# Two more one-class gemm1 blocks in the fill list, a later start for the last output projection, and a guard on pulling class-0 tiles

## The chip, the cores and the metric

The kernel runs on one core of a Trainium2 chip. The metric is device time in microseconds (us) of one execution. Five engines work side by side, each through its own queue in order: TensorE (PE, with its weight loads as PEld), VectorE (DVE), ScalarE (ACT), GpSimd (POOL) and SyncE (SP, which here only issues DMAs). A tile framework inserts the semaphores; it also lists the instructions of each engine, by the order in which the program emits them where they are ready in its own reckoning.

## The reference

Two kinds of layer alternate, twice each, on x of 2048 positions by D = 1024 (bf16):

```python
x = x + A(layernorm(x), wqkv, wo)        # attention, 32 heads of 32
x = x + B(layernorm(x), w1, b1, w2, b2)  # MLP across positions, F = 3584
...
# A: each position attends to W = 8 positions, a distance dil = 2 apart:
idx = pos[:, None] - dil * arange(8)[None, :]
logits = einsum("bhsd,bhswd->bhsw", q, k[idx]) * scale    # masked where idx < 0
o = einsum("bhsw,bhswd->bhsd", softmax(logits), v[idx])   # then o @ wo
# B: normalises x again, then mixes the positions of each channel:
u = gelu(einsum("bsd,sf->bdf", layernorm(x), w1) + b1)
y = einsum("bdf,fs->bds", u, w2) + b2                     # then transposed back
```

## The kernel before, in words

Because the window has a step of 2, the even positions ("class 0") and the odd ones ("class 1") never meet in attention. Each class has 1024 rows, that is 8 tiles of 128. One pass of the loop over `li` ("layer 0", "layer 1" below) does an attention layer and the MLP that follows.

**Attention.** TensorE projects q, k and v (`project`, L410) and ScalarE copies them out of PSUM (L414, L417). For each chunk n of four 128-row groups (chunks 0 and 1 are class 0, chunks 2 and 3 class 1) VectorE multiplies q by shifted k into a tile T (`qk`, L442), TensorE sums over the head with 8 narrow matmuls ("sc", L447), `softmax_front` and `softmax_back` follow, a DMA spreads the probabilities into `pb`, and VectorE forms the weighted sum of v in `pv` (L503 to L509), whose result is oT. T tiles share 2 buffers, so a third T waits for the sc matmuls of the first.

**Output projection.** `out_proj` multiplies oT by wo for 8 tiles, each in two PSUM banks (n = 0, 1) of 8 matmuls (kt = 0 to 7; L629); VectorE adds the residual and so frees the bank (L650 or L653), POOL writes the row tile to `xa`, and the tile is normalised into h2. wo comes in four DMAs of 512 KB (L619). For class 1 the first three tiles are begun early: kt 0 to 5 of all three, which fills the 6 banks of the pool `psp`, then kt 6 and 7 tile by tile.

**gemm1.** The 3584 columns of w1 are 14 blocks (`fb`) of 256, each in 4 units (2 column tiles by 2 halves of D). A unit over one class is 8 matmuls (L680), over both 16. Blocks 0 to NPART-1 = 9 are done class by class: the class-0 partial sum is copied to g by ScalarE (L686), and later VectorE adds the class-1 sum to it (L691) before the gelu (L692). Blocks 10 to 13 take both classes at once (gelu straight from PSUM, L688). The g of blocks 6 to 13 lie in the memory of v of class 1 (`v_g`). A class of a block needs its own w1 tile (L667, 512 KB). w1, w2, wo and some wqkv tiles share the five buffers of `wbp`. `gemm2_tile` (L704, L709) does the second MLP product.

**Order around the change.** `weave` writes the order. The `lead` is the attention stream and then `out_proj` of class 1. The `fills` are class-0 `out_proj` ("out0"), the class-0 partials of gemm1 blocks 0 to 5 ("partials") and of blocks 6 to NPART-1 ("late"), besides `second` and `v_ahead`. `weave` keeps two planned clocks, `pe` and `dve`; each unit says its cost. Before a lead unit that needs TensorE at time t, `reach(t)` pulls fill units until pe is within SLACK = 0.5 of t or none is open. A DVE unit of the lead also pulls one out0 tile (3.5 of pe) whenever another OUT0_GAP = 7.0 of DVE cost has gone by. What is left of the fills is pulled after the lead. Early class-1 accumulation waits, by the entry `("less", "oT", -6.0)`, until pe is at the planned end of the last `pv` plus 6.

Of the kernel before, what the change touches and what calls it, by code (L numbers as in the profile page):

```python
# [13 lines left out]
BF16 = mybir.dt.bfloat16  # L14

P = 128
# [3 lines left out]
DIL = 2  # L20
# [6 lines left out]
def kernel(  # L27
# [13 lines left out]
    nc = tc.nc  # L41
# [3 lines left out]
    F = B_w1.shape[1]  # L45
    KD = D // P
    FT = F // P
    SC = S // DIL
    NT = SC // P
    HT = SC // 2  # L50
    NDC = D // 512
# [8 lines left out]
    FB = 256  # L60
    NFB = F // FB
    GF = FB // P
    NPART = 10
    NW2 = 4
    HF = FT // NW2
    SLACK = 0.5
    PB_LAG = 12.0
    PDW = 4 * SB * W * TB + 512
    OUT0_GAP = 7.0
    assert D == H * DH and W == 8 and SC == 1024 and HD * KD == H and SB * CH == 32  # L70
    scale = float(DH) ** -0.5

    def pool(name, bufs, **kw):
        return ctx.enter_context(tc.tile_pool(name=name, bufs=bufs, **kw))
# [8 lines left out]
    tpl = pool("tpl", 2)  # L83
    pbp = pool("pbp", 2)
    otp = pool("otp", KD)
    dram = pool("dram", 1, space=bass.MemoryType.DRAM)
# [19 lines left out]
    def bank(name="ps"):  # L106
        return psp.tile([P, 512], FP32, name=name, tag="ps")
# [4 lines left out]
    def hx(name, shape):  # L112
        return hxp.tile(shape, BF16, name=name, tag="hx")

    def wb(name, shape):
        return wbp.tile(shape, BF16, name=name, tag="wb")
# [53 lines left out]

    xa = [[dram.tile([SC, D], BF16, name=f"xa{li}{c}") for c in range(DIL)] for li in range(2)]
    xb = [dram.tile([SC, D], BF16, name=f"xb{c}") for c in range(DIL)]
    pd = [dram.tile([CH, PDW], BF16, name=f"pd{n}") for n in range(2 * DIL * NCQ)]

    xin_v = x_in.rearrange("(i m c) d -> c i m d", m=P, c=DIL)
# [6 lines left out]
    def rows(t):  # L182
        return t.rearrange("(i m) d -> i m d", m=P)
# [425 lines left out]
    def out_proj(at_, c, res, dst, h2, on_act):  # L609

        early = 0 if on_act else 3
        if early:
            yield "pe", 1.28 * early * NDC, [("oT", 0), ("less", "oT", -6.0)], [], 0.0
        dst_v = rows(dst)
        wo_t = [[None, None] for _ in range(NDC)]
        for n in range(NDC):
            for hf in range(2):
                wt = wb("wo", [P, KD // 2, 512])
                nc.sync.dma_start(out=wt[:], in_=wo_v[hf, :, :, n * 512:(n + 1) * 512])  # L619
                wo_t[n][hf] = wt  # L620
        for hf in range(2):
            h2[c][hf] = hx(f"h2{c}{hf}", [P, NT // 2, D])
        banks = {}

        def multiply(i, n, kts):
            if (i, n) not in banks:
                banks[(i, n)] = bank()
            for kt in kts:
                nc.tensor.matmul(banks[(i, n)][:], lhsT=at_.oT[c][kt][:, i * P:(i + 1) * P],  # L629
                                 rhs=wo_t[n][kt // 4][:, kt % 4, :], start=(kt == 0), stop=(kt == KD - 1))  # L630

        def kts(i):
            return range(KD - 2 if i < early else 0, KD)

        for i in range(early):
            for n in range(NDC):
                multiply(i, n, range(KD - 2))
        xrs = Rows([res[i] for i in range(NT)], 2)
        for i in range(NT):
            if early:  # L640
                yield "pe", 0.43 * len(kts(i)), ["oT"], [], 3.6
                on_act = i % 2 == 0
            xn = xrs.take()
            s1 = st("s1", [P, NDC]) if on_act else None
            for n in range(NDC):
                cols = slice(n * 512, (n + 1) * 512)
                multiply(i, n, kts(i))
                ps = banks.pop((i, n))
                if on_act:
                    nc.vector.scalar_tensor_tensor(out=xn[:, cols], in0=ps[:], scalar=1.0, in1=xn[:, cols], op0=ALU.mult,  # L650
                                                   op1=ALU.add, accum_out=s1[:, n:n + 1])
                else:
                    nc.vector.tensor_tensor(out=xn[:, cols], in0=ps[:], in1=xn[:, cols], op=ALU.add)  # L653
            nc.gpsimd.dma_start(out=dst_v[i], in_=xn[:])
            h = h2[c][i // 4][:, i % 4, :]
            if on_act:
                nm, rs = stats_act(xn[:], 1.0 + EPS, eps2, h, s1)
                norm_act(h, xn[:], nm, rs)
            else:
                mean, rs = stats_dve(xn[:], 1.0 + EPS, eps2)  # L660
                norm_dve(h, xn[:], mean, rs)
            if not early:
                yield 3.5, 0.0
# [31 lines left out]
    def gemm2_tile(c, i, w2t, xs, dst, hT, on_act=False, end=False):  # L695
        xo = xs.take()
        halves = [slice(n * 512, (n + 1) * 512) for n in range(NDC)]
        groups = [halves[:1], [slice(512, 768)], [slice(768, 1024)]] if end else [halves]
        for cols in groups:
            acc = [bank() for _ in cols]  # L700
            for n in range(NW2):
                for ft in range(n * HF, (n + 1) * HF):
                    for ps, xc in zip(acc, cols):
                        nc.tensor.matmul(ps[:, 0:xc.stop - xc.start], lhsT=w2t[n][:, ft % HF, c::DIL],  # L704
                                         rhs=g[ft // GF][:, ft % GF, xc], start=(ft == 0), stop=(ft == FT - 1))
                if n < NW2 - 1:
                    yield 1.5 * len(cols), 0.0
            for ps, xc in zip(acc, cols):
                nc.vector.scalar_tensor_tensor(out=xo[:, xc], in0=ps[:, 0:xc.stop - xc.start], scalar=b2_sb[:, i, c:c + 1],  # L709
                                               in1=xo[:, xc], op0=ALU.add, op1=ALU.add)  # L710
            yield 1.5 * len(cols), 0.75 * len(cols)
            if end:
                nc.sync.dma_start(out=dst[:, cols[0]], in_=xo[:, cols[0]])
        if not end:
            nc.gpsimd.dma_start(out=dst, in_=xo[:])
        if hT is None:
            return
        hb = x2("hb")
        if on_act:
            nm, rs = stats_act(xo[:], 1.0, eps1, hb[:])  # L720
            norm_act(hb[:], xo[:], nm, rs)
        else:
            mean, rs = stats_dve(xo[:], 1.0, eps1)
            norm_dve(hb[:], xo[:], mean, rs)
        to_hT(hb[:], hT, c, i)
        yield 0.0, 0.0 if on_act else 2.0

    def w2_tiles(i):
        tiles = []
        for n in range(NW2):  # L730
            t = wb("w2", [P, HF, FB])
            nc.sync.dma_start(out=t[:], in_=w2_v[:, n * HF:(n + 1) * HF, i * FB:(i + 1) * FB])
            tiles.append(t)
        return tiles

    def run(*its):
        for _ in chain(*its):
# [2 lines left out]
    def weave(lead, fills, lags):  # L740


        pe = dve = due = 0.0
# [32 lines left out]
        for kind, *unit in lead:  # L776
            if kind == "open":
                after = {"out0": "oT", "partials": "out0", "late": "out0", "v_ahead": "second"}.get(unit[0])
                opened[unit[0]] = when.get(after, float("inf")) if after else pe
            elif kind == "drain":  # L780
                while unit[0] in opened:
                    pull(True)
            elif kind == "at":
                pe, dve = unit
            elif kind == "pe":
                cost, waits, sets, then = unit
                reach(ready(pe, waits))
                pe += cost
                when.update((x, pe + 2.0) for x in sets)
                if then:  # L790
                    dve = max(dve, pe) + then
            else:
                cost, waits, sets, lag, then = unit
                dve = ready(dve, waits) + cost
                if then:
                    reach(dve)
                    pe += then
                when.update((x, dve + lag) for x in sets)
                if list(opened)[:1] == ["out0"] and opened["out0"] < pe:
                    due += cost  # L800
                    if due > OUT0_GAP:
                        due -= OUT0_GAP
                        pull()
        while pull(True):
# [4 lines left out]
    for li in range(2):  # L809
# [39 lines left out]
        def partials(lo, hi):  # L849
            for fb in range(lo, hi):  # L850
# [4 lines left out]
                     "out0": out_proj(at_, 0, res[0], xa[li][0], h2, on_act=True),  # L855
                     "partials": partials(0, NFB - KD), "late": partials(NFB - KD, NPART)},
              {"second": 25.0} if first else {})
        for fb in range(NPART, NFB):
            run(gemm1(h2, fb, (0, 1), True, True))
        for fb in range(NPART):  # L860
            run(gemm1(h2, fb, (1,), False, True))
# [8 lines left out]
        else:  # L870
            xs = Rows([rows(xa[1][c])[i] for i in range(NT) for c in range(DIL)], 1)
            for i in range(NT):
                w2t = w2_tiles(i)
# [32 lines left out]
```

## Time and profile before

| | |
|---|---|
| median of 3 runs | 1305.59 us (1304.1 to 1305.82) |
| profiled execution, its own time | 1303.7 us |
| its span, first to last instruction | 1301.9 us |
| PE busy | 1274.3 us (98%), 6284 matmuls |
| DVE busy | 669.5 us (51%) |
| ACT busy | 463.9 us (36%) |
| mean granted TensorE clock | 0.997 |
| DMA | 173.00 MB, mean 133 GB/s |

The span has a part for layer 0 up to about 575 us and one for layer 1 after it. In the timeline each row gives start, duration, engine, line, operation, output<-input and the number of instructions merged; a bracket says how long the engine was idle before it and what released it. In a table of windows each engine has its busy time in the stretch and, in brackets, its number of instructions; PEclk is the granted share of TensorE's full clock.

### The profile page before, as it was taken

The page shows a single profiled execution, that of the slowest core. Times are in us where ns is not written, and L with a number is a line of the kernel's source. Part 1 is how long each engine was busy: PE and PEld are TensorE (multiplying, and loading weights), DVE is VectorE, ACT ScalarE, POOL GpSimd, SP SyncE. Part 2 cuts the span into 40 slices and gives each one's busy share as a digit, 9 for nine tenths or more (in the row PEclk, how much of TensorE's full clock was granted, in tenths as well). Part 3 has the DMA queues.
Part 4 walks back from the last instruction along what each step waited for, and adds up shares of the span by engine and source line. Part 5 has one row for each costly group of instructions (what it writes and reads, how often), then busy time and mean ns, then how long its engine had stood idle before and what let it go on. Part 6 is the DMA issues. An engine that isn't in the chain of part 4 may idle for free. (4 is left out here: it accounts for less than half of the span.)

```text
span 1301.9 us, 15529 instructions
## 1 busy us (share of the span) xinstructions
PE 1274.3 (98%) x6284; PEld 575.2 (44%) x6284; DVE 669.5 (51%) x845; ACT 463.9 (36%) x788; POOL 60.8 (5%) x166
## 2 busy tenths in 40 slices
PE   8999999998999999999999999999999999999999
PEld 4344444443444444444444444444444444444444
DVE  6879899988003423335896734879920044011011
ACT  6845447634313410024414535475352244000000
POOL 3000001001000000000000000010000000000000
PEclk9999999998999999999999999999999999999999
DMA  9843436653422268753659772338252321434331
GB/s 257 181 121 97 106 105 170 172 136 107 135 66 81 75 156 225 213 144 109 165 160 239 188 203 65 90 122 226 81 172 62 92 81 57 135 112 131 113 112 53
DMA packets 243544, 173.00 MB, mean 133 GB/s; under 512 B 32208, under 2 KB 227152, under 8 KB 241424
## 3 DMA queue, kind: packets, MB, share of 16 engines
q1 hardware_dynamic: 233648, 133.45, 38.1%
q0 software_dynamic: 9248, 37.51, 10.2%
q8 instruction: 49, 0.80, 0.3%
q10 hardware_dynamic: 576, 1.05, 0.2%
q14 instruction: 23, 0.19, 0.0%
HBM read 146.81 MB, written 18.87 MB: 127 GB/s over the span
## 5 line engine op out<-in xcount | busy, mean ns | idle before, releaser
L704 PE MATMUL ps<-g,w 128*128 128x512 bf16 (+1 forms) x1820 | 390.7, 376 | 3.4 <-ACT v L417 2.2
L680 PE MATMUL ps<-h,w 128*128 128x512 bf16 x1792 | 388.9, 379 | 4.3 <-ACT h L231 3.0
L704 PEld LDWEIGHTS <-w 128*128 128x128 bf16 x1820 | 177.4, 98 | 215.0 <-issue 6.9
L680 PEld LDWEIGHTS <-w 128*128 128x128 bf16 x1792 | 175.0, 98 | 217.4 <-issue 6.0
L410 PE MATMUL ps<-hT,wq 128*128 128x512 bf16 (+1 forms) x1112 | 243.4, 375 | 3.5 <-DVE xr L709 2.2
L691 DVE TENSOR_TENSOR tmp<-ps,g 128x512 f32<-128x512 f32 x80 | 55.4, 692 | 232.8 <-PE ps L680 232.8
L709 DVE SCALAR_TENSOR_TENSOR xr<-ps,b_sb,xr 128x512 bf16<-128x512 f32 (+1 forms) x65 | 45.6, 737 | 251.7 <-PE ps L704 211.8
L442 DVE TENSOR_TENSOR T<-q,k 128x4096 bf16<-128x4096 bf16 x60 | 135.5, 2285 | 63.5 <-ACT q L414 52.9
L410 PEld LDWEIGHTS <-wq 128*128 128x128 bf16 x1112 | 108.4, 100 | 133.1 <-issue 15.0
L507 DVE TENSOR_TENSOR pr<-pr 128x2048 bf16<-128x2048 bf16 (+1 forms) x128 | 119.1, 945 | 0.2
L410 PE MATMUL ps<-hT,wv 128*128 128x512 bf16 x448 | 101.8, 380 | 0.0
L629 PE MATMUL ps<-wo,oT 128*128 128x512 bf16 x384 | 90.5, 382 | 1.6 <-DMA wo<-in_A_wo_dram 1.6
L417 ACT CAST k<-ps 128x1024 bf16<-128x1024 f32 x60 | 60.8, 1015 | 76.6 <-PE ps L410 74.6
L503 DVE TENSOR_TENSOR pr<-pb,v 128x2048 bf16<-128x2048 bf16 x64 | 76.0, 1215 | 23.2 <-DMA pb<-pd 13.5
L692 ACT ACTIVATE g<-tmp,b_sb 128x512 bf16<-128x512 f32 x80 | 57.7, 722 | 82.1 <-DVE tmp L691 82.1
L503 DVE TENSOR_TENSOR pr<-pb,g 128x2048 bf16<-128x2048 bf16 x64 | 76.2, 1212 | 9.0 <-DMA pb<-pd 9.0
L686 ACT CAST g<-ps 128x512 bf16<-128x512 f32 x80 | 45.8, 591 | 73.3 <-PE ps L680 73.3
L410 PEld LDWEIGHTS <-wv 128*128 128x128 bf16 x448 | 48.6, 112 | 50.5 <-issue 7.2
L629 PEld LDWEIGHTS <-oT 128*128 128x128 bf16 x384 | 37.4, 98 | 48.7 <-issue 5.1
L688 ACT ACTIVATE g<-ps,b_sb 128x512 bf16<-128x512 f32 x32 | 22.0, 687 | 83.2 <-PE ps L680 83.2
L414 ACT CAST q<-ps 128x512 bf16<-128x512 f32 x60 | 34.8, 584 | 46.7 <-PE ps L410 46.7
L417 ACT CAST g<-ps 128x1024 bf16<-128x1024 f32 x36 | 36.6, 1017 | 40.6 <-PE ps L410 40.6
(90 smaller groups left out, 597.6 us busy)
## 6 DMA issues: line engine op xcount, KB each, us to landing
w<-in_B_w_dram SPq DMA_DIRECT2D x96, 448.0 KB, 3.7
w<-in_B_w_dram SPq DMA_DIRECT2D x56, 512.0 KB, 4.5
wq<-in_A_wqkv_dram SPq DMA_DIRECT2D x38, 512.0 KB, 4.2
pb<-pd POOLq DMA_DIRECT2D x16, 1024.0 KB, 10.1
wo<-in_A_wo_dram SPq DMA_DIRECT2D x16, 512.0 KB, 5.1
xa<-xr POOLq DMA_DIRECT2D x32, 256.0 KB, 3.3
xr<-xa SPq DMA_DIRECT2D x32, 256.0 KB, 3.6
wv<-in_A_wqkv_dram SPq DMA_DIRECT2D x14, 512.0 KB, 6.9
```

The source lines that it names most:

```text
L410: nc.tensor.matmul(ps[:, lo:hi], lhsT=cols, rhs=self.hT[c][hf][:, kt, lo:hi], start=(kt == 0), stop=(kt == KD - 1))
L417: nc.scalar.copy(out=window(buf, 0, PADK + hf * HT, [(KW + 1, 2), (1, HT)]), in_=ps[:].unsqueeze(1).to_broadcast([P, 2, HT]))
L442: nc.vector.tensor_tensor(out=T[:], in0=q.unsqueeze(1).to_broadcast([P, 4, SC]), in1=window(k, par, 2, [(2, 4), (1, SC)]), op=ALU.mult)
L503: nc.vector.tensor_tensor(out=pr[:, :, u, :], in0=pb[:, :, u, :], in1=window(self.v_of(c, dt), par, 2 + hf * HT, [(TB, 4), (2, 4), (1, TB) ...
L507: nc.vector.tensor_tensor(out=pr[:, :, 0:wd, :], in0=pr[:, :, 0:wd, :], in1=pr[:, :, wd:2 * wd, :], op=ALU.add)
L629: nc.tensor.matmul(banks[(i, n)][:], lhsT=at_.oT[c][kt][:, i * P:(i + 1) * P], rhs=wo_t[n][kt // 4][:, kt % 4, :], start=(kt == 0), stop=( ...
L680: nc.tensor.matmul(ps[:], lhsT=wt[c][:, i, fl * P:(fl + 1) * P], rhs=h2[c][i // 4][:, i % 4, dc * 512:(dc + 1) * 512], start=(k == 0), sto ...
L686: nc.scalar.copy(out=gs, in_=ps[:])
L691: nc.vector.tensor_tensor(out=tmp[:], in0=ps[:], in1=gs, op=ALU.add)
L692: nc.scalar.activation(out=gs, in_=tmp[:], func=ACT.Gelu_apprx_tanh, bias=b1_sb[:, ft:ft + 1])
L704: nc.tensor.matmul(ps[:, 0:xc.stop - xc.start], lhsT=w2t[n][:, ft % HF, c::DIL], rhs=g[ft // GF][:, ft % GF, xc], start=(ft == 0), stop=(f ...
L709: nc.vector.scalar_tensor_tensor(out=xo[:, xc], in0=ps[:, 0:xc.stop - xc.start], scalar=b2_sb[:, i, c:c + 1], in1=xo[:, xc], op0=ALU.add, ...
```

## The change

Three things act. NPART becomes 12, so blocks 10 and 11 of gemm1 are done class by class as well, in both layers, and their class-0 partials join the "late" fills; only blocks 12 and 13 take both classes at once. The wait of the early class-1 accumulation is for the planned end of the last `pv` plus 12, no longer plus 6. And a class-0 output tile that is due in a DVE unit of the lead is not pulled while pe is AHEAD = 10 or more ahead of dve; it stays due, and the next DVE unit asks again.

The rest doesn't act: gemm2 takes its w2 slice through a function that gives the same slice as before, and `keep`, `w2_kept` and the DRAM tiles `w2_odd` are defined but no caller uses them (the calls of `w2_tiles(i)` in L840, L869 and L873 are as they were).

```diff
-    NPART = 10
+    NPART = 12
...
     OUT0_GAP = 7.0
+    AHEAD = 10.0
...
+    w2_odd = [dram.tile([P, F], BF16, name=f"w2o{i}") for i in range(NT)]
...
         if early:
-            yield "pe", 1.28 * early * NDC, [("oT", 0), ("less", "oT", -6.0)], [], 0.0
+            yield "pe", 1.28 * early * NDC, [("oT", 0), ("less", "oT", -12.0)], [], 0.0
...
-                        nc.tensor.matmul(ps[:, 0:xc.stop - xc.start], lhsT=w2t[n][:, ft % HF, c::DIL],
+                        nc.tensor.matmul(ps[:, 0:xc.stop - xc.start], lhsT=w2t(ft, c),
...
-    def w2_tiles(i):
+    def w2_tiles(i, keep=False):
         tiles = []
+        odd = tpl.tile([P, NW2, HF, P], BF16, name="odd", tag="T") if keep else None
         for n in range(NW2):
             t = wb("w2", [P, HF, FB])
             nc.sync.dma_start(out=t[:], in_=w2_v[:, n * HF:(n + 1) * HF, i * FB:(i + 1) * FB])
+            if keep:
+                nc.scalar.copy(out=odd[:, n], in_=t[:, :, 1::DIL])
             tiles.append(t)
-        return tiles
...
+        return lambda ft, c: tiles[ft // HF][:, ft % HF, c::DIL]
+
+    def w2_kept(i):
...
                 if list(opened)[:1] == ["out0"] and opened["out0"] < pe:
                     due += cost
-                    if due > OUT0_GAP:
+                    if due > OUT0_GAP and pe < dve + AHEAD:
                         due -= OUT0_GAP
                         pull()
```

More of the change, by code (lines that the diff above doesn't have):

```diff
@@ L732, in w2_tiles @@
             nc.sync.dma_start(out=t[:], in_=w2_v[:, n * HF:(n + 1) * HF, i * FB:(i + 1) * FB])
+            if keep:
+                nc.scalar.copy(out=odd[:, n], in_=t[:, :, 1::DIL])
             tiles.append(t)
-        return tiles
+        if keep:
+            nc.scalar.dma_start(out=w2_odd[i].rearrange("p (f m) -> p f m", m=P), in_=odd[:].rearrange("p n f m -> p (n f) m"))
+        return lambda ft, c: tiles[ft // HF][:, ft % HF, c::DIL]
+    def w2_kept(i):
+        tiles = []
+        for n in range(2):
+            t = wb("w2", [P, FT // 2, P])
+            nc.sync.dma_start(out=t[:].rearrange("p f m -> p (f m)"), in_=w2_odd[i][:, n * F // 2:(n + 1) * F // 2])
+            tiles.append(t)
+        return lambda ft, c: tiles[ft // (FT // 2)][:, ft % (FT // 2), :]
     def run(*its):
```

## The prediction

> **What bounds the kernel now.** I read the page first: PE is busy 98% of the span. The rest, 1301.9 - 1274.3 = 27.6 us, and time lost to a lower clock is all that an edit which adds and removes no matmul can win. This one has 6284 before and after: a gemm1 block has 4 x 16 matmuls whether it takes the classes together or apart. So I looked for where PE stands, in a table of windows:
>
> ```profile
> 290.00:300.00 10.00, 9.36 (x44) 4.13 (x43) 10.00 (x12) 0.00 (x0) 0.00 (x0) 1.00 0.00 0
> 300.00:310.00 10.00, 5.97 (x18) 2.31 (x18) 9.49 (x22) 5.15 (x13) 1.67 (x3) 0.66 0.20 59
> ...
> 880.00:890.00 10.00, 9.19 (x43) 4.00 (x41) 10.00 (x17) 5.21 (x12) 1.74 (x3) 1.00 0.99 270
> 890.00:900.00 10.00, 8.24 (x40) 3.63 (x38) 7.38 (x9) 7.26 (x15) 1.05 (x2) 1.00 0.80 210
> ```
>
> (Busy us and count of PE, PEld, DVE, ACT, POOL; then PEclk, DMA share, GB/s.) Two places lie in what `weave` orders. At 300 us, in layer 0, PE is idle and then has a clock of 0.66. At 880 to 893, in layer 1, it has small gaps. The others (the opening, q/k/v of layer 0, 675 to 775) lie ahead of anything that changes in their layer.
>
> PE's timeline at the first, with DVE's:
>
> ```profile
> 296.17 3.19 PE L629 MATMUL ps<-wo,oT 128*128 128x512 bf16 x14
> 304.03 1.87 PE L629 MATMUL ps<-wo,v 128*128 128x512 bf16 x4 [4.67 <-DVE xr L650]
> 305.69 1.91 PE L629 MATMUL ps<-wo,oT 128*128 128x512 bf16 x4
> 307.39 1.59 PE L629 MATMUL ps<-wo,v 128*128 128x512 bf16 x4
> 308.82 1.03 PE L629 MATMUL ps<-wo,oT 128*128 128x512 bf16 x4
> ...
> 326.35 18.95 PE L680 MATMUL ps<-h,w 128*128 128x512 bf16 x87 [0.96 <-DMA w<-in_B_w_dram]
> ```
> ```profile
> 302.94 0.42 DVE L509 TENSOR_TENSOR oT<-pr 128x512 bf16<-128x512 bf16 x1
> 303.28 0.69 DVE L650 SCALAR_TENSOR_TENSOR xr<-ps,xr 128x512 bf16<-128x512 f32 x1
> ```
>
> The three early class-1 tiles fill all 6 PSUM banks. They are done by 299.4, but the evictions that free the banks stand in DVE's queue behind the last `pv`, which ends at 303.3. Tile 3 waits 4.67 us for a bank. Only work put ahead of the early tiles fills that time: a unit of gemm1 needs a bank too.
>
> At the second place (PE, DVE, ACT):
>
> ```profile
> 885.05 2.75 PE L680 MATMUL ps<-h,w 128*128 128x512 bf16 x12 [0.47 <-ACT h L231]
> 888.14 3.18 PE L680 MATMUL ps<-h,w 128*128 128x512 bf16 x14 [0.34 <-DVE xr L650]
> 893.08 32.54 PE L680 MATMUL ps<-h,w 128*128 128x512 bf16 x150 [1.76 <-ACT h L231]
> ```
> ```profile
> 864.86 0.69 DVE L650 SCALAR_TENSOR_TENSOR xr<-ps,xr 128x512 bf16<-128x512 f32 x1 [1.03 <-PE ps L629]
> ...
> 865.49 4.49 DVE L442 TENSOR_TENSOR T<-q,k 128x4096 bf16<-128x4096 bf16 x2
> ```
>
> PE has begun gemm1 in all its banks and waits for h2 of the last class-0 tile, written on ACT at 893.0. The chain of waits leads back from there through ACT and a DVE without a gap to the T at 867.7. Ahead of that, at 852 to 865, DVE waited 9.3 us for PE in 8 pieces: four class-0 output tiles stood in PE's queue ahead of the sc matmuls that free T's buffers.
>
> **The later start (+12 for +6), with NPART.** `weave` pulls units of 8 x 0.216 = 1.728 of pe until pe is within 0.5 of the target. In layer 0 its clocks stand at pe 245.0 and dve 292.2 after the last `pv`: (292.2 + 6 - 0.5 - 245.0) / 1.728 = 30.5, so 31 units. The trace has 248 L680 matmuls ahead of the early tiles, which is 31 x 8, so this arithmetic can be trusted for order. With 12: 33.97, so 34 units. In layer 1 (pe 326.4, dve 359.7; one unit is drained earlier) 24 become 27, three of them block 6 from "late"; 192 matmuls in the trace confirm the 24. So 3 more units, 3 x 8 x 0.216 = 5.18 us of PE work, go ahead of the early tiles in each layer.
>
> Layer 0: the early tiles begin at 288.83 + 5.18 = 294.0 and PE asks for tile 3's bank at 299.36 + 5.18 = 304.54. DVE frees it at 303.97 as before. The stall of 4.67 us goes, with 0.5 us to spare. After it 12 matmuls took 304.03 to 308.82, 4.79 us, where 12 x 0.216 = 2.59 was due: 2.20 us more. [...] By the row the place is worth 4.67 + 2.20 = 6.87 us[...]. I take the row, since my sum is against this execution[...]. Next late is DVE, 6 evictions behind, but a tile takes DVE some 2.5 us (2 x 0.69, and 2.1 more for every other tile) against 3.46 on PE. Tile 4's residual comes at about 308.6 + 3.2 = 311.8, and the bank that waits for it isn't asked for before 318. PE stays fed.
>
> Weight DMAs. The fourth wo tile takes the buffer of a w1 tile that ends 2 units, 3.46 us, before the early start (before: 3 units; its DMA at 283.8 landed in 3.7). It is used 10 matmuls, 2.2 us, into the early tiles: 5.6 us of time against 3.7. I take 0. With the slowest landing of the four, 11.2, it is 5.6, a bound I think far: that one met `pb` traffic, this one runs alone. After class 1's last tile PE waited 0.96 us for w1, since one unit was left of the block at hand. Now two are left, 1.73 us more: -0.96. In layer 1 the roles change: 27 units leave just one, where 24 ended a block whose successor's w1 had long been loaded. I take the same 0.96 there, as +0.96 (0 to 2). In layer 1 nothing else waited but some 0.15 us at 935.98 for a bank, which goes: -0.15.
>
> **NPART's other half.** Per layer 8 units more go through ACT's copy (8 x 0.59 = 4.7 us) and DVE's add (8 x 0.69 = 5.5 us), with the w1 loads the same in number. They lie in stretches in which PE has 1.73 us per unit against 0.69 of DVE and 0.72 + 0.59 of ACT, and PE shows no gap from 345 to 550. Taken at 0; without that cover 8 x 1.3 = 10 us per layer. Blocks 10 and 11 overwrite v that the last `pv` has read long before.
>
> **AHEAD.** By the planner's clocks a gate needs pe 10 ahead of dve at a pull. Layer 0's widest is 219.1 against 210.1, 9.0: nothing changes. Layer 1 has 291.7 against 277.6 and, later, 299.3 against 289.2: two pulls are put off by one DVE unit each, and tile 3 falls behind the first sc group of chunk 3's second half. On PE that group moves up by one tile, 16 x 0.216 = 3.46 us, from 864.8 to about 861.3; its T has been ready since 848. The next T begins at about 862 in place of 865.5; the one after is held by tile 3 and the second sc group until about 865.8, where it stood at 867.7. So DVE's tight run begins 1.8 us earlier, less up to 1 us if it then stands for tile 4's second bank at 870.0. I take 1.2, and as that run sets h2, PE's gaps fall from 2.57 to 1.4. Both sides: -2.57 (gaps gone) to +2 (the framework lists DVE's work otherwise and h2 comes later). The moved tiles' xr loads on SP and xa writes on POOL go with them and stand ahead of the pb writes as before.
>
> **Sum.** Layer 0: -6.87 - 0.96 = -7.83. Layer 1: -1.2 - 0.15 + 0.96 = -0.4. Together -8.2. The profiled execution, 1303.7 (span 1301.9 and 1.8 around it), becomes 1295.5. It was 1.9 below the median of the runs; on the median I predict 1305.6 - 8.2 = 1297.4.
>
> **Rivals.** About 0.2%, 2.6 us, is what a measurement of this kernel can tell from none.
> 1. [...]4.67 + 0.96 + 0.4 = 6.0 to 7, so 1299.
> 2. The place at 300 takes a new wait. For: a wo tile's landing reached 11.2; then 5.6 of 6.87 comes back, and 1303.0 to 1304 remains. Against: 3.7 on the quiet queue.
> 3. Layer 1 wins all its gaps and w1 comes in time: another 1.4 + 0.96, so 1295.
> 4. Slower: the gate postpones DVE's evictions. If both postponed tiles push the last class-0 eviction behind one more `pv` unit each (2 x 4.4 us, by the row spacing of `pv` at 904 to 935), h2 comes 8.8 us later, and PE, with its banks all begun, stands over 11 us and loses 2.2 to the clock: -8.2 + 1.2 + 8.8 + 2.2 = +4, 1309.6. It decides where h2 is over 7.4 us late. Against: the late pulls catch up by the second T, ahead of DVE's tight run.
> 5. The units don't go ahead since the framework lists them elsewhere: 1305. Against: 31 and 24 hold.
>
> **How the numbers follow.** Forecast (with 1) 0.68, rival 3 0.10, rival 2 and 5 together 0.13, rival 4 0.09. Faster 0.78, within 0.2% 0.13, slower 0.09. The range runs from rival 3, with 1 us of spread, to the faster edge of rival 2: 1294 to 1303.
>
> **What would show it.** Right: 272 and 216 L680 matmuls ahead of the early tiles, no wait on L650 over 1 us and a clock of 1.00 near 305, the T run of layer 1 beginning near 862, a w1 wait of about 1 us after layer 1's projection and none in layer 0. Wrong: a wait on wo near 296, h2 of layer 1 later than 893, or a PE gap in gemm1's class-1 pass.

## The result, and the profile after

The changed kernel takes 1296.56 us in the median (1295.91 to 1298.79, 4 runs) against 1304.96 for the kernel before (1304.1 to 1305.82, 4 runs). The ratio is 0.9939, 95% interval 0.9921 to 0.9956: faster by 8 us. The forecast was 8.2. A second group of runs, beside other kernels, gave 0.9941 (0.9928 to 0.9953).

The same windows of the profile after, with the columns as in the prediction. The lines of the code have moved by 2, so L629 is now L631, L650 is L652 and L680 is L682:

```profile
290.00:300.00 10.00, 9.95 (x47) 4.53 (x47) 10.00 (x12) 2.34 (x4) 0.00 (x0) 1.00 0.18 52
300.00:310.00 10.00, 9.95 (x48) 4.51 (x47) 9.96 (x21) 3.59 (x8) 1.13 (x2) 1.00 0.14 52
870.00:880.00 10.00, 8.96 (x42) 3.99 (x41) 9.91 (x17) 7.42 (x15) 0.88 (x2) 1.00 0.91 261
880.00:890.00 10.00, 9.59 (x45) 4.29 (x45) 9.28 (x13) 7.37 (x16) 1.92 (x4) 1.00 0.79 222
```

At 300 us PE is full and its clock is 1.00. Windows that read 9.95 are full as well: this trace lacks some matmul records (6163 of 6284), so counts are taken from PEld. A table for the gemm1 line alone (PE, PEld, then clock, DMA share, GB/s), up to the early class-1 tiles of each layer, shows how many matmuls now lie ahead of them:

```profile
220.00:295.30 75.30, 59.23 (x266) 26.34 (x272) 1.00 0.56 150
845.00:922.50 77.50, 46.70 (x212) 21.13 (x216) 1.00 0.59 164
```

There are 272 and 216 weight loads, that is 34 and 27 units, as forecast. PE's timeline at the place where it stood idle, and at its end:

```profile
302.65 3.19 PE L631 MATMUL ps<-wo,oT 128*128 128x512 bf16 x14
305.68 1.03 PE L631 MATMUL ps<-wo,v 128*128 128x512 bf16 x3
306.54 1.03 PE L631 MATMUL ps<-wo,oT 128*128 128x512 bf16 x4
...
322.94 22.39 PE L682 MATMUL ps<-h,w 128*128 128x512 bf16 x101
```

Tile 3 follows the early tiles without a bracket, and gemm1 follows the last tile without one. In layer 1:

```profile
877.77 6.85 PE L682 MATMUL ps<-h,w 128*128 128x512 bf16 x30 [1.04 <-ACT h L233]
884.98 37.72 PE L682 MATMUL ps<-h,w 128*128 128x512 bf16 x171 [0.36 <-ACT h L233]
...
950.15 1.89 PE L682 MATMUL ps<-h,w 128*128 128x512 bf16 x8
952.76 12.48 PE L682 MATMUL ps<-h,w 128*128 128x512 bf16 x56 [0.72 <-DMA w<-in_B_w_dram]
```

The gaps for h2 are 1.40 us, and one unit after the class-1 projection PE waits for w1, which it did in layer 0 before.

What the gate moved shows in DVE's timeline, counted from the start of the class-0 projection on PE. That start, in the kernel before, is

```profile
850.19 2.75 PE L629 MATMUL ps<-wo,oT 128*128 128x512 bf16 x12
```

so the T at 865.49, shown in the prediction, began 15.3 us after it. In the changed kernel it is 11.9 us:

```profile
843.44 2.75 PE L631 MATMUL ps<-wo,oT 128*128 128x512 bf16 x12
...
855.33 2.29 DVE L444 TENSOR_TENSOR T<-q,k 128x4096 bf16<-128x4096 bf16 x1
```

The two traces can be set against each other by the start and end of the same work on PE. Where the changed kernel has 3 units more (or fewer) in a stretch, 5.18 us are taken off (or added):

| stretch on PE | before | after, same work | difference | forecast |
|---|---|---|---|---|
| start to layer 0's early tiles | 288.83 | 295.32 - 5.18 | +1.31 | 0 |
| early tiles to end of that projection | 34.67 | 27.62 | -7.05 | -6.87 |
| from there to layer 1's class-0 projection | 526.69 | 520.50 + 5.18 | -1.01 | -0.96 |
| from there to layer 1's early tiles | 75.26 | 79.09 - 5.18 | -1.35 | -1.2 |
| early tiles to end of that projection | 27.80 | 27.62 | -0.18 | -0.15 |
| from there to the end | 348.65 | 344.35 + 5.18 | +0.88 | +0.96 |
| span | 1301.9 | 1294.5 | -7.4 | -8.2 |

### The profile page after: what moved, and what is told of

It reads as the page before. It is cut to its first block, busy times and chain, and to the rows that moved or that the text cites. A ratio compares the mean times of both kernels' runs of the same rounds, so it can differ in the third digit from the quotient of the medians.

```text
span 1294.5 us, 15457 instructions
## 1 busy us (share of the span) xinstructions
PE 1264.3 (98%) x6163; PEld 574.5 (44%) x6284; DVE 680.3 (53%) x861; ACT 473.5 (37%) x804; POOL 60.8 (5%) x166
## 5 line engine op out<-in xcount | busy, mean ns | idle before, releaser
L682 PE MATMUL ps<-h,w 128*128 128x512 bf16 x1756 | 386.7, 379 | 4.7 <-ACT h L233 2.1
L682 PEld LDWEIGHTS <-w 128*128 128x128 bf16 x1792 | 175.0, 98 | 215.8 <-issue 4.6
L693 DVE TENSOR_TENSOR tmp<-ps,g 128x512 f32<-128x512 f32 x96 | 66.4, 692 | 209.8 <-PE ps L682 205.6
L694 ACT ACTIVATE g<-tmp,b_sb 128x512 bf16<-128x512 f32 x96 | 69.2, 721 | 98.2 <-DVE tmp L693 98.2
L631 PE MATMUL ps<-wo,oT 128*128 128x512 bf16 x377 | 89.1, 379 | 2.6 <-DMA wo<-in_A_wo_dram 2.2
L688 ACT CAST g<-ps 128x512 bf16<-128x512 f32 x96 | 55.1, 589 | 90.2 <-PE ps L682 84.4
L631 PEld LDWEIGHTS <-oT 128*128 128x128 bf16 x384 | 37.3, 98 | 48.6 <-issue 4.5
L449 PE MATMUL sc<-T,sel 128*32 128x512 bf16 x512 | 38.6, 383 | 4.9 <-DVE T L444 4.7
```

The costliest lines, as they stand in the source:

```text
L449: nc.tensor.matmul(self.sc[32 * gr:32 * gr + 32, par], lhsT=sel[:, sb * DQ + dq, :], rhs=T[:, :, b * TB:(b + 1) * TB], start=(dq == 0 and ...
L682: nc.tensor.matmul(ps[:], lhsT=wt[c][:, i, fl * P:(fl + 1) * P], rhs=h2[c][i // 4][:, i % 4, dc * 512:(dc + 1) * 512], start=(k == 0), sto ...
L688: nc.scalar.copy(out=gs, in_=ps[:])
L693: nc.vector.tensor_tensor(out=tmp[:], in0=ps[:], in1=gs, op=ALU.add)
L694: nc.scalar.activation(out=gs, in_=tmp[:], func=ACT.Gelu_apprx_tanh, bias=b1_sb[:, ft:ft + 1])
```

## The experiments

The kernel before ran beside each group: 40 runs with the first four, 18 with the next four, 9 with the last three.

**1 to 4: one part at a time.** All start from the changed kernel.

```diff
e1 (none):    NPART = 10, AHEAD = 1e9, ("less", "oT", -6.0)
e2 (later):   NPART = 10, AHEAD = 1e9
e3 (blocks):  AHEAD = 1e9, ("less", "oT", -6.0)
e4 (gate):    NPART = 10, ("less", "oT", -6.0)
```

> The changed kernel with all three active edits undone (10 blocks, +6, no gate); the unused code stays. Theory (each part does what its step said, and the 1.3 us that the profiled run of after lost ahead of 290 us is scatter): no difference, ratio 1.000, the 4.7 us wait on a bank and the low clock near 300 are back, the L680-type matmuls ahead of the early class-1 tiles are 248 and 192. Rival (the unused code or its DRAM tiles cost or win something): a ratio off by over 0.2%.

Measured 1305.28 us, ratio 0.9993 (0.9982 to 1.0005). The unused code costs nothing that shows. In its profile the early tiles of layer 0 begin at 291.0, against 288.8 in the profile of before, with the same work ahead of them. With the moved units taken off, this start lies between 288.8 and 293.6 in the 13 profiles, so the +1.31 of the table's first row is scatter.

> Only +12 in place of +6; 10 blocks, no gate. Theory: it carries nearly all: layer 0 -7.8 us, layer 1 -0.15 and +0.7 to 1.0 for a w1 wait after the class-1 projection, so about -7 us, ratio 0.9946; PE gaps at h2 of layer 1 stay at 2.6 us. Rival (12 blocks are needed, since the fills would run out): less than half of it, ratio above 0.997.

Measured 1298.87 us, ratio 0.9952 (0.9934 to 0.9969): most of the gain, with 10 blocks. The h2 gaps are the 2.6 us of before, the bank wait is gone, the w1 wait in layer 1 is 0.80.

> Only 12 blocks in place of 10; +6, no gate. Theory: nothing, ratio 1.000 within 0.1%: 31 and 24 units ahead of the early tiles as before, the 4.7 us wait stays, and the 16 more copies and adds lie under PE. Rival 1 (more blocks ahead is what fills the wait): ratio 0.995. Rival 2 (the copies and adds cost): up to 1.3 us per unit, 1.016.

Measured 1305.45 us, ratio 1.000 (0.999 to 1.0011), with 248 and 192 matmuls ahead of the early tiles. Neither rival holds: two blocks more in the list put nothing ahead, and their 16 copies and 16 adds cost nothing that the runs resolve.

> Only the gate of 10; 10 blocks, +6. Theory: layer 0 unchanged; in layer 1 the PE gaps waiting for class-0 h2 fall from 2.6 us to about 1.4, so -1.2 us, ratio 0.999. Rival (the gate carries the gain, or delays h2): a ratio off by more than 0.3%, with PE gaps near 880 of 0 or of over 4 us.

Measured 1306.78 us, ratio 1.0002 (0.9994 to 1.0011). The forecast step is there and its gain isn't. The h2 gaps fall to 1.4, as forecast (PE's timeline):

```profile
886.47 6.85 PE L682 MATMUL ps<-h,w 128*128 128x512 bf16 x31 [1.04 <-ACT h L233]
893.68 32.53 PE L682 MATMUL ps<-h,w 128*128 128x512 bf16 x150 [0.36 <-ACT h L233]
939.07 1.02 PE L631 MATMUL ps<-wo,v 128*128 128x512 bf16 x4 [2.50 <-DVE xr L652]
```

But PE, now 1.3 us earlier, stands 2.50 us for a bank at class-1 tile 3, where it hardly stood before (0.15 us, by the spacing of its matmuls). What held DVE, from 840 us (845 in before) to 905, by the view of waits, first in the kernel before and then in e4:

```profile
DVE xr L650 <- PE ps L629: 9.3, 8, 1.7
DVE pr L503 <- DMA pb<-pd: 2.6, 1, 2.6
```
```profile
DVE xr L652 <- PE ps L631: 7.9, 7, 1.8
DVE pr L505 <- DMA pb<-pd: 5.1, 1, 5.1
```

(Total us, times, longest.) DVE waits 1.4 us less for PE, and then 2.5 us more for the spread probabilities. So its last `pv`, and with it the bank, comes 1.2 us later than before (87.0 us after the start of the class-0 projection on PE, against 85.8). In the profiles of the kernels with a gate of 10 this wait is 4.4 to 5.1 us, without a gate 2.2 to 2.6. The pb transfer that DVE waits for took 9.2 us to land, against 7.3 before, and in the 26 us from 886 the queue of the other loads moved 3.47 MB beside it, against 2.89. That the sharing of the DMA engines is the cause wasn't tried. In the profile the gate alone thus wins 1.3 us and loses 2.5; the runs, at 1.0002, fit anything from 0.8 us won to 1.4 us lost.

**5 and 6: how many units it takes, and what the clock does.**

```diff
e5:  ("less", "oT", -8.0)
e6:  ("less", "oT", -18.0)
```

> The changed kernel with +8 in place of +12: 32 and 25 units ahead of the early tiles (34 and 27 in after). One unit more than before in layer 0, 1.73 us, should leave a wait on a bank of 4.7 - 1.7 = about 3 us there. Theory (the clock falls only after a gap as long as the 4.7 to 5.2 us ones; the 2.5 us gap of the gate-only run kept its clock): no low clock, so one unit wins 1.7 + 2.2 = 3.9 us of the 6.9, and no w1 wait after either class-1 projection (0 and 3 units left of a block); 3.0 - 0.7 = 2.3 us above after, ratio to before about 0.9957. Rival (any wait there costs the clock): 4.5 us above after, ratio 0.9974.

Measured 1301.97 us, ratio 0.9975 (0.9967 to 0.9982): the theory's 0.9957 lies outside the interval, the rival's 0.9974 inside. PE's timeline:

```profile
304.92 1.02 PE L631 MATMUL ps<-wo,v 128*128 128x512 bf16 x4 [2.96 <-DVE xr L652]
305.78 1.59 PE L631 MATMUL ps<-wo,oT 128*128 128x512 bf16 x4
307.17 1.91 PE L631 MATMUL ps<-wo,v 128*128 128x512 bf16 x4
308.88 1.34 PE L631 MATMUL ps<-wo,oT 128*128 128x512 bf16 x4
310.05 1.03 PE L631 MATMUL ps<-wo,v 128*128 128x512 bf16 x4
```

The wait is 2.96 us as forecast, but the clock falls after it too: the first 16 of these matmuls take 5.13 us where 3.46 are due, 1.67 lost. The rest of the distance to the changed kernel lies in layer 1, which has 25 units: a bank wait of 0.68 us, which I had not expected, and no w1 wait (0.72 less). 2.96 + 1.67 + 0.68 - 0.72 = 4.6 us, or 0.35%, as measured. So "any wait costs the clock" isn't shown either: e4's 2.50 us wait in layer 1 was followed by matmuls at full speed.

The 13 profiles show where it falls. In all that have it, the clock of 0.50 comes in pieces of 3.41 us, one or two together (the first and last microseconds of the span aside): 6.83 us in before, 301.69 to 308.52, and 3.41 us in e5, from 306.10. Two falls in one profile lie a whole number of such pieces apart (in e2 at 105.19 and 193.94 us, 26 pieces). So in these profiles the clock goes by steps of 3.41 us, and their place in the kernel differs from execution to execution: 301.69 and 306.10 lie 4.41 us apart. In a table of windows cut at these steps, counted in each profile from its own falls:

| profile | step | PE busy, us | clock in it | clock in the next |
|---|---|---|---|---|
| before | 298.28 to 301.69 | 1.08 | 1.00 | 0.50 |
| before | 301.69 to 305.10 | 1.07 | 0.50 | 0.50 |
| before | 305.10 to 308.52 | 3.42 | 0.50 | 1.00 |
| e5 | 302.69 to 306.10 | 1.18 | 1.00 | 0.50 |
| e4, layer 1 | 934.45 to 937.86 | 2.12 | 1.00 | 1.00 |
| e4, layer 1 | 937.86 to 941.28 | 2.21 | 1.00 | 1.00 |

Between 8 and 1290 us the 13 profiles have 16 falls. The step ahead of each has PE busy for 0.15 to 1.52 of its 3.41 us. Of the steps at full clock that no fall follows, two have 1.46 and 1.48 (e4, e9), all others 1.57 or more. So in these profiles a fall comes where PE is idle for some 1.9 us or more of one step. The 2.50 us of e4 were split between two steps, 1.3 and 1.2 us. A wait of 4.67 us, however it lies, leaves at least 2.3 us idle in one step, so it should cost the clock in every execution: my estimate from these 16 falls, for this place.

The profiles bear it out: near 300 us the clock falls in all five with a wait there (before, e1, e3, e4, e5) and in none of the eight in which it is covered. The mean granted clock that each run lists can't tell this. It is 0.999 for e5's profiled execution, which has the fall at 300, and 0.997 for e2's, which hasn't but has two others. Nine of the 13 profiles have falls near 40, 105 or 193 us, which add to the scatter of the profiles: in e7 and e10 the 33 matmuls from 193 us on took 8.97 us, the same 33 in e8 7.28, so 1.69 us lost.

> The changed kernel with +18 in place of +12: 38 and 31 units ahead. Theory (the wait is covered by 3 units, more only moves work): the same as after within 0.1%, ratio 0.994; w1 waits as in after, since 2 and 1 units of a block are left again. Rival (what stands before the early tiles is held up by weights, so that more of it costs, or by 3 units the wait was not yet covered in most runs): over 0.15% off after.

Measured 1296.0 us, ratio 0.9936 (0.9917 to 0.9954): equal to after. It has 38 and 31 units ahead: four more win nothing and cost nothing. In layer 1 DVE now stands 8.8 us for PE once, at the end of `pv`: it is DVE that has slack.

**7 and 8: can the two small waits that are left be won?**

```diff
e7:  AHEAD = 6.0
e8:  ("less", "oT", -12.0 - at_.li)
```

> The changed kernel with a gate of 6 in place of 10: five pulls put off, one of them in layer 0, and the second sc group of chunk 3's second half leaves PE ahead of tile 3. Theory (DVE's run in layer 1 begins when the sc groups are done): T begins up to 3 us earlier, the PE gaps for h2 in layer 1 fall from 1.4 to under 0.7, 0.5 to 1.4 us below after, ratio 0.993. Rival (the tiles' own matmuls or the pb transfer then hold DVE): gaps of 1.4 or more, no gain or a loss up to 2 us.

Measured 1296.77 us, ratio 0.9939 (0.9922 to 0.9955): no gain. The first T after class-0 tiles begins 3.5 us earlier in relation to the projection's start than in after, as expected; the gap for h2 is one of 1.48 us. It is for tile 6, and it ends with that tile's last step on ACT (ACT's timeline):

```profile
873.85 0.20 ACT L196 ACTIVATE rs<-ln 128x1 f32<-128x1 f32 x1
874.08 0.29 ACT L232 ACTIVATE bi<-nm,rs 128x1 f32<-128x1 f32 x1
874.41 1.24 ACT L233 ACTIVATE h<-xr,bi,rs 128x1024 bf16<-128x1024 bf16 x1
875.55 0.19 ACT L219 ACTIVATE t<-s 128x1 f32<-128x1 f32 x1
...
878.26 1.24 ACT L233 ACTIVATE h<-xr,bi,rs 128x1024 bf16<-128x1024 bf16 x1
```

Rows follow each other without a bracket: 3.85 us of ACT a tile, against 3.46 of PE. My theory falls and so do the rival's two causes: with DVE out of the way, ACT's normalisation is next. (The rival's numbers, a gap of 1.4 or more and no gain, are met.)

> The changed kernel with +13 in layer 1 alone: 28 units there end a block, and the next block's w1 can load ahead of the wo tiles. Theory: the w1 wait of 0.7 us after layer 1's class-1 projection goes, nothing else moves, 0.7 us below after, ratio 0.9934. Rival (the wait is the queue's, not the count's): it stays at 0.7.

Measured 1295.81 us, ratio 0.9934 (0.9915 to 0.9953). The wait for w1 after layer 1's class-1 projection is gone from the profile, and with it 0.9 us of the last stretch. That is below what the runs resolve.

**9 to 11: the changed kernel beside two variants.**

```diff
e9:   (the changed kernel)
e10:  NPART = 10
e11:  ("less", "oT", -12.0 - at_.li)     (e8 again)
```

> The changed kernel once more, beside the two others of this group. Theory: ratio to before 0.9935 to 0.9945, the three PE waits as in its first profile (no bank wait near 300, 1.4 us for h2 of layer 1, 0.7 us for w1 after the class-1 projection of layer 1). Rival (its first runs were a lucky day): above 0.9955.

> The changed kernel with 10 blocks done class by class in place of 12; +12 and the gate stay. Theory (34 and 27 units are asked for and 40 are there, so blocks 10 and 11 are never reached ahead of the early tiles): equal to the changed kernel run beside it within 0.1%. Rival (with the gate or with +12 the two blocks do count): 0.15% or more above it.

> The kernel of e8 (+13 in layer 1, +12 in layer 0) again, to be set against the changed kernel on one chip. Theory: the 0.7 us wait for w1 is gone in the profile, 0.05% below the changed kernel run beside it, which the runs may not resolve. Rival: equal or above, the time being taken again elsewhere.

Measured 1297.52, 1297.21 and 1297.06 us; ratios 0.9941 (0.9928 to 0.9953), 0.9938 (0.9926 to 0.9951) and 0.9941 (0.9928 to 0.9955). The two extra blocks don't count with the other parts present either. e11 has no w1 wait in its profile and is not measurably faster. No version tried beats the changed kernel by more than the scatter.

## Why the prediction was right, point by point

**The later start.** Right in count and size: 3 units in each layer, the bank wait gone, -7.05 against -6.87 in that stretch. e2 shows that it carries most of the gain by itself, e3 and e10 that the number of blocks has no part in it. The 0.5 us to spare were not there: in e2 and e7 the stretch takes 27.77 us in place of 27.63, so the wait is covered only just.

**The clock.** I took the row, 2.20 us, since my sum was against that execution. The size was right: the four profiles with a wait of 4.7 to 5.2 us lost 1.9 to 2.6 beside it. Rival 1, which has the wait of 4.67 us without these 2.20, is out: all five profiles with a wait near 300 have the fall. That most runs would be spared it was a guess of mine that no run shows. My own rule in e5, that only the long gaps cost the clock, fell as well: 2.96 us cost 1.67.

**Weight DMAs.** Right in both places: layer 0 has no w1 wait after the change, and +0.96 became a wait of 0.72. The table's -1.01 is no measure of the first, since the same stretch, with the moved units added, takes 523.5 to 527.2 us in the other profiles. e8 shows that the count of units left of a block decides it. The tightened wo load in layer 0 did not hold PE.

**The blocks' other half.** Right at 0 (e3).

**The gate.** The mechanism and the PE gaps were right: 2.57 to 1.40 us, T begins 3.4 us earlier where 3.5 was worked out. What I missed is that the step wins nothing by itself. I followed DVE's earlier run to h2, but not on to its next wait, for pb, which grew by more than DVE had won. The bank then comes 1.2 us later than before, and PE gives 2.50 us back at class-1 tile 3 (e4). With the later start PE asks 5.18 us later, and the gain is kept. The profiles agree on it: from the class-0 projection to the early tiles, with the moved units taken off, PE takes 73.8 to 74.0 us in the eight with a gate of 10 and 75.3 to 75.4 in the four without, and with the later start the projection then takes 27.6 in both kinds. The runs fit, e2 at 0.9952 and after at 0.9939 to 0.9941, without resolving it. That the -1.2 came true in the whole was luck: my list had it as if it stood alone, and it depends on the later start. The -0.15 was scatter, since e1 and e3 take 27.63 us for that projection with no such wait.

**The sum.** -8.2 forecast, -7.4 in the profiled pair, of which +1.31 is scatter ahead of the change, and 8.0 by the ratio. The rival that was slower (h2 late by two `pv` units) did not occur: h2 came earlier.

## What to carry to other kernels

An engine that is 98% busy can still have one place worth an edit; there, count what has to be ahead of the blocking step, in units whose cost the trace shows, and stop when it is covered: one unit of three won 3 of the 8 us and left the clock's fall, and seven won no more than three. Follow an engine that is made earlier past the first consumer to its own next wait, since a gain can be taken back there until another edit gives that place slack. Where several constants change at once, undo them one by one: here one carried most, one works only beside it, and the one that the title names first did nothing.

## What the runs showed of the hardware that was not expected

The length of a PE wait did not decide alone whether the clock fell: after 2.00 us for wo near 193 in e10 it did (33 matmuls in 8.97 us), after 2.27 us at the same place in e8 it did not (7.28). After PE waits of 4.7 to 5.2 us near 300, as in before, e1, e3 and e4, the matmuls that followed took about 0.42 us in place of 0.216 for some 3.5 to 5 us. After 2.96 us (e5) they started at full speed, fell to the same rate about 1 us later and lost 1.67 us in all; after 2.50 us (layer 1 of e4) nothing fell. What these 13 profiles have in common is the idle time that falls into one step of 3.41 us, about 1.9 us or more (16 falls, PE busy 1.52 us or less in the step ahead), not the length of the gap. Whether the exact limit lies at PE busy of 1.46 or of 1.52 us they leave open, since matmul ends are modelled and some records are missing.
